# Chunked decay attention before a two-layer MLP and an expert layer: state, output and the next block's masked scores in one visit of TensorE

## The chip, the cores and the metric

One NeuronCore of a Trainium2 chip runs the whole program in one launch. The metric is the device time of that launch in microseconds (us). The engines are TensorE (PE; its weight loads are PEld), VectorE (DVE), ScalarE (ACT), GpSimd (POOL) and SyncE (SP, which here only issues loads).

## The reference

Three stages. The first is attention with a decay: for each head the sequence of 768 is cut into blocks, and a state of 64 x 64 per head runs through them.

```
intra = (q_b k_b^T * Dmask) v_b            # Dmask[i,j] = lam^(i-j) for i >= j
inter = (q_b * lam^(i+1)) kv_state
out_b = intra + inter
kv_state = lam^block * kv_state + (k_b * lam^(block-1-j))^T v_b
```

The second is an MLP over 1536 tokens, 512 to 2048 to 512, with the activation (h+1)^2/4 between -1 and 1, 0 below and h above. The third picks one of 8 experts for each token by the scaled dot product of the normalised token with the expert's embedding, applies a 512 to 1024 to 512 MLP with ReLU, and multiplies by the gate. The kernel uses blocks of 128, which gives the same function: 6 blocks for each of 2 sequences, 12 in all, m = 0 to 11. Blocks 0 and 6 start a sequence (cb = 0, no state comes in); blocks 5 and 11 end one (cb = 5, no state goes out).

## The kernel before, in words

**Order of work.** Layer 1 (the MLP) is a list of units (1, c, g): three chunks c of four blocks (512 tokens), eight groups g of 256 hidden columns. Units 0 to 7 are chunk 0, 8 to 15 chunk 1, 16 to 23 chunk 2; then come the expert tiles. In unit n TensorE does `m1_l1(n, 0)` and `m1_l1(n, 1)` (12 matmuls each, tile `l`), then the second layer of the unit before, `m1_l2(n - 1, j)` for j = 0 to 3 (6 matmuls each, tile `acc`). Every product is made of three matmuls, high and low halves of values and weights.

**Attention among the units.** Blocks 0 to 4 (`NSTART` = 5) run ahead of everything. Blocks 5 to 11 are needed by chunks 1 and 2 and are put between the matmuls of layer 1: `plan` holds functions by quarter steps, and `place(n, k)` runs them behind the first half (k = 0), the second half (1), the second layer's j = 1 (2) and j = 3 (3) of unit n. `attn_pieces` makes the pieces of a block: `prep` (GpSimd's kd and qd, and the loads of the next block on SyncE, L273 to L296), `masked` (score matmuls L308 in tile `sc`, mask multiplication L311 on VectorE to `am`), `outv` and `outs` (output matmuls L335 and L348 in tile `ao`, their eviction L354 on ScalarE and L355 on VectorE), `st` (state matmuls L377 in tile `as`, the new state L380 on ScalarE or four L383 on VectorE). `scores` is `prep` and `masked`. Blocks 5 to 7 are spread over steps 0.5 to 7.75, blocks 8 to 11 over 8.5 to 15.75, each as [scores, st, output, nothing].

**Who decides the order.** TensorE's order is the order in which the program issues it (`manual_schedule`). VectorE, ScalarE, GpSimd and SyncE get a fixed order when the program is compiled: a planner goes through a simulated time and takes for each engine the instruction earliest in the program whose inputs it thinks ready. On the chip each engine runs its list in order and waits where an input is late.

**Banks.** Accumulators `acc0` to `acc3` take four banks, `ps_l1` two (tag `l1`, the two halves of a layer-1 unit), `ps_at` two (tag `at`, all attention tiles and small ones). A layer-1 bank is free again when ScalarE has read it (L719, then L720 squares in place) and VectorE has made `g_t` from both (L722); `gh` (L726) and `gl` (L727) follow. `kd` and `qd` have two buffers each, `am` three; attention inputs have two buffers (`big_a`, `big_b`).

**Weights.** In chunk 0 the raw 8-byte weights are converted by ScalarE and VectorE (`convert`, L223 to L239; cu, cz, cw) and stored for the later chunks; `hilo` (L212, L213) splits them. For unit n this is issued ahead of the unit's matmuls. Chunk 0's tokens are scored against the experts during units 9 to 12 (L449 on VectorE, eight for each block, tile `jk` with the tag `kd`).

Of the kernel before, what the change touches and what calls it, by code (L numbers as in the profile page):

```python
# [8 lines left out]
F32 = mybir.dt.float32  # L9
# [8 lines left out]
P = 128  # L18
NTOK = 1536
DM = 512  # L20
NBLK = 12
NE = 8
TMAX = 13
CHUNKS = [4, 4, 4]
# [7 lines left out]

X2STEP = (1.0, 0.75)
ROUTE = (6.5, 4.5)
SPREAD = (0.5, 7.75)

WARM = 11
NSTART = 5
WARM_LAM = 6

SWAP = 7
# [6 lines left out]
def kernel(  # L48
# [15 lines left out]
    V, A, G, PE, SP = nc.vector, nc.scalar, nc.gpsimd, nc.tensor, nc.sync  # L64
# [8 lines left out]
    ps_l1 = ctx.enter_context(tc.tile_pool(name="ps_l1", bufs=2, space=bass.MemoryType.PSUM))  # L73
# [179 lines left out]
    first_blk = []  # L253
# [4 lines left out]
    ast = {}  # L258
    pieces = {}
# [3 lines left out]
    def at_tile(shape, name):  # L263
        if at_tags:
            pool, tag = at_tags.popleft()
            return pool.tile(shape, F32, name=name, tag=tag)
        return ps_at.tile(shape, F32, name=name, tag="at")

    def attn_pieces(m):
        c, j = blk_chunk[m]  # L270
        cb = m % 6

        def prep():  # L273
            if m >= NSTART - 1 and m + 1 < NBLK:
                load_attn(m + 1)
            qkt, kvt = attn_in[m]
            def keys():
                kd = sb.tile([P, NE, 64], F32, name="kd", tag="kd")
                G.tensor_tensor(kd, kvt[:, 0], rev.to_broadcast([P, NE, 64]), op=ALU.mult)
                ast[m, "kd"] = kd  # L280


            if cb < 5 and m >= NSTART:
                keys()
            if cb > 0:
                qd = sb.tile([P, 4, P], F32, name="qd", tag="qd")
                if m < SWAP:
                    G.tensor_tensor(qd, qkt[:, 0], wq, op=ALU.mult)
                else:
                    G.tensor_tensor(qd[:, 0::2, :], qkt[:, 0, 0::2, :], wq[:, 0::2, :], op=ALU.mult)  # L290
                    for h2 in range(2):
                        r, o = slice(64 * h2, 64 * h2 + 64), slice(64 - 64 * h2, 128 - 64 * h2)
                        G.tensor_tensor(qd[o, 1::2, :], qkt[r, 0, 1::2, :], wq[r, 1::2, :], op=ALU.mult)
                ast[m, "qd"] = qd
            if cb < 5 and m < NSTART:
                keys()  # L296

        def scores():
            prep()
            masked()  # L300

        def masked():
            qkt, kvt = attn_in[m]
            pts = [at_tile([P, 4, P], "sc") for _ in range(2)]
            for pr in range(4):
                for h2 in range(2):
                    r = slice(64 * h2, 64 * h2 + 64)
                    PE.matmul(pts[h2][:, pr, :], lhsT=qkt[r, 1, pr, :], rhs=qkt[r, 0, pr, :], start=True, stop=True)  # L308
            for h2 in range(2):
                am = sb3.tile([P, 4, P], F32, name="am", tag="am")  # L310
                ast[m, "am"] = V.tensor_tensor(am, pts[h2], dmask.rearrange("p (r o) i -> p r o i", o=2)[:, :, h2, :], op=ALU.mult)  # L311
                ast[m, "A", h2] = am

        def outv():
            kvt = attn_in[m][1]
            if j == 0:
                n = CHUNKS[c]
                xh[c] = sb.tile([P, 4, n * P], F32R, name="xh", tag="xh")
                xl[c] = sb.tile([P, 4, n * P], F32R, name="xl", tag="xl")
            am = [ast.pop((m, "A", i)) for i in range(2)]  # L320


            if m < SWAP:
                pt = at_tile([P, 4, P], "ao")
                pts, first, last = [pt[:, pr, :] for pr in range(4)], (0,), (3,)
                ast[m, "o"] = pts, [(pt, slice(0, 4))]
            else:
                two = [at_tile([P, 2, P], "ao") for _ in range(2)]
                pts, first, last = [two[pr % 2][:, pr // 2, :] for pr in range(4)], (0, 1), (2, 3)
                ast[m, "o"] = pts, [(two[i], slice(i, 4, 2)) for i in range(2)]  # L330
            ast[m, "last"] = last
            for pr in range(4):
                for h2 in range(2):
                    r = slice(64 * h2, 64 * h2 + 64)
                    PE.matmul(  # L335
                        pts[pr][r], lhsT=kvt[:, 1, 2 * pr + h2, :], rhs=am[h2][:, pr, :],
                        start=(pr in first), stop=(cb == 0 and pr in last), skip_group_check=True,
                    )

        def outs():  # L340
            pts, banks = ast.pop((m, "o"))
            last = ast.pop((m, "last"))
            if cb > 0:
                for pr in range(4):
                    for h2 in range(2):
                        r = slice(64 * h2, 64 * h2 + 64)
                        w = r if m < SWAP or pr % 2 == 0 else slice(64 - 64 * h2, 128 - 64 * h2)
                        PE.matmul(  # L348
                            pts[pr][r], lhsT=state[m - 1][w, pr, :], rhs=ast[m, "qd"][w, pr, :],
                            start=False, stop=(pr in last), skip_group_check=True,  # L350
                        )
            sl = slice(j * P, (j + 1) * P)
            for pt, prs in banks:
                ast[m, "xh"] = A.activation(xh[c][:, prs, sl], pt, AF.Copy)  # L354
                ast[m, "xl"] = V.tensor_tensor(xl[c][:, prs, sl], pt, xh[c].bitcast(F32)[:, prs, sl], op=ALU.subtract)  # L355

        def outp():
            outv()
            outs()

        def st():
            if m == NSTART:
                with tc.issue_after(ast[m, "am"].ins):
                    V.tensor_copy(lamx[:, 0::2], lamc[:, 0::2])
                    V.tensor_copy(lamx[64:128, 1::2], lamc[0:64, 1::2])
                    V.tensor_copy(lamx[0:64, 1::2], lamc[64:128, 1::2])
            if cb == 5:
                return
            qkt, kvt = attn_in[m]
            kd = ast.pop((m, "kd"))  # L370
            pt = at_tile([P, 4, 64], "as")
            for pr in range(4):
                for h2 in range(2):
                    h = 2 * pr + h2
                    at_ = 64 * h2 if m < SWAP - 1 or pr % 2 == 0 else 64 - 64 * h2
                    r = slice(at_, at_ + 64)
                    PE.matmul(pt[r, pr, :], lhsT=kd[:, h, :], rhs=kvt[:, 1, h, :], start=True, stop=True)  # L377
            sn = sb.tile([P, 4, 64], F32, name="s_new", tag="state")
            if cb == 0:
                A.activation(sn, pt, AF.Copy)  # L380
            else:
                for pr in range(4):
                    V.scalar_tensor_tensor(  # L383
                        sn[:, pr, :], state[m - 1][:, pr, :], (lamc if m < SWAP else lamx)[:, pr, :], pt[:, pr, :], op0=ALU.mult, op1=ALU.add,
                    )
            state[m] = sn

        pieces[m] = (prep, masked, outv, outs)
        return [scores, st, outp, None] if m >= NSTART else [scores, None, outp, st]


    def inv_norm(s, n, nm, over_=None):
# [440 lines left out]
    pcs = [attn_pieces(m) for m in range(NBLK)]  # L833
# [8 lines left out]
    for h2 in range(2):  # L842
        PE.matmul(
            lps[64 * h2:64 * h2 + 64, NE:NE + 4], lhsT=ident[:, P - 1:P].to_broadcast([P, 64]),
            rhs=rev.rearrange("p (r h) o -> p r (h o)", h=2)[:, :, h2], start=True, stop=True,
# [4 lines left out]
    for h2 in range(2):  # L850
        PE.matmul(
            wqp[64 * h2:64 * h2 + 64], lhsT=ident[:, P - 1:P].to_broadcast([P, 64]),
            rhs=dmask.rearrange("p (r o) i -> p r o i", o=2)[:, :, h2, :], start=True, stop=True,
# [25 lines left out]
    def at(step, *fs):  # L879

        s0 = round(4 * step)
        for i, f in enumerate(fs):
            if f:
                plan.setdefault(s0 + i, []).append(f)

    def spread(fs, s0, s1):
        for i, f in enumerate(fs):
            at(s0 + (s1 - s0) * i / len(fs), f)

    def place(n, k):  # L890
        now[0] = n + k / 4.0
        for f in plan.pop(4 * n + k, ()):
            f()
# [62 lines left out]
    for n in range(NU):  # L956
        lay, c, g = units[n]
        if lay == 1 and g == 0:
            if c + 1 < len(CHUNKS):
                m0 = first_blk[c + 1]  # L960
                fs = [f for m in range(max(m0, NSTART), m0 + CHUNKS[c + 1]) for f in pcs[m]]
                spread(fs, n + SPREAD[0], n + SPREAD[1])
            if c == 1:
                setup_routing()
        load_w(1, n + 2)
# [90 lines left out]
    with tc.If(lo_n < hi_n):  # L1056
        with tc.For_i(lo_n, hi_n) as i:
            e = SP.value_load(eti[0:1, bass.ds(i, 1)], min_val=0, max_val=NE - 1)
            dyn = []
            for nm, src in (("ixd", idx), ("rowd", row), ("gxd", gx)):  # L1060
                d = sb.tile([P, 2], I32, name=nm, tag=nm)
# [74 lines left out]
```

## Time and profile before

| | |
|---|---|
| Median of 3 runs | 476.63 us (474.26 to 476.95) |
| The profiled execution | 474.53 us, span of the instructions 472.7 us |
| TensorE | 463.7 us busy (98%), 2713 matmuls |
| VectorE | 326.7 us (69%) |
| ScalarE | 266.6 us (56%) |
| GpSimd | 82.4 us (17%) |
| Mean granted TensorE clock | 0.996 |

Rows of a timeline are: start, duration, engine, line, operation, output <- inputs, shape, count, and in brackets idle time before it with what ended it. Matmuls are pipelined: a row's duration is longer than its distance to the next, and distances are what counts. A 4-byte matmul of attention shows as two records, so eight matmuls are x16. A row of waits is: who <- whom, us in total, times, longest.

### The profile page before, as it was taken

The numbers are of one execution on the slowest core, as the hardware profiler recorded it, in microseconds if no ns is written. First come the engines' busy times: TensorE is split into PE (matmuls) and PEld (weight loads), VectorE is DVE, ScalarE is ACT, GpSimd is POOL, SyncE is SP. The second block draws the span as 40 slices with busy tenths as digits, with TensorE's granted clock in tenths as the row PEclk, the third lists the DMA queues.
The fourth block names the chain that finished last, engine by engine and source line by source line (L and its number), as shares of the span: only waits on it lengthen the run. The fifth ranks groups of instructions, "written<-read, shape, count | busy, mean of one in ns | idle before, by whom it ended". The sixth has DMA issues, their size and how long they took to land.

```text
span 472.7 us, 7356 instructions
## 1 busy us (share of the span) xinstructions
PE 463.7 (98%) x2713; PEld 377.7 (80%) x2713; DVE 326.7 (69%) x725; ACT 266.6 (56%) x403; POOL 82.4 (17%) x83
## 2 busy tenths in 40 slices
PE   8999999999999999999999999999999999999994
PEld 5875878878878787878888888887778889899882
DVE  6889889879399997474799875575794445435430
ACT  2388879868874454454665655556433534533521
POOL 4612420002003030000000005200055600500202
PEclk9999999999999999999999999999999999999998
DMA  8999987868563333122423325240275633543401
GB/s 327 420 411 367 392 305 287 298 231 251 230 220 137 97 128 116 63 90 90 178 67 125 122 90 179 90 155 23 88 250 178 201 136 109 179 155 98 146 1 50
DMA packets 22651, 83.65 MB, mean 177 GB/s; under 512 B 3595, under 2 KB 3595, under 8 KB 20564
## 3 DMA queue, kind: packets, MB, share of 16 engines
q1 hardware_dynamic: 15842, 65.04, 38.9%
q10 hardware_dynamic: 4322, 11.55, 6.2%
q0 software_dynamic: 2448, 6.56, 4.0%
q8 instruction: 22, 0.36, 0.3%
q14 instruction: 17, 0.14, 0.1%
HBM read 68.44 MB, written 14.73 MB: 176 GB/s over the span
## 4 chain that ended last, share of the span: by engine, by line
PE 68%; issue 20%; POOL 6%; DVE 3%; ACT 1%; POOLq 0%; another core or an unknown queue 0%; ACTq 0%
PE l L700 10%; PE acc L743 9%; PE l L702 9%; PE acc L744 9%; PE l L703 9%; PE acc L745 9%; POOL out_dram L823 2%; PE ao L335 2%; PE sc L308 2%; POOL xg L763 2%; POOL gate L771 2%; PE acc L738 1%; PE ao L348 1%; PE as L377 1%; PE m L794 1%
## 5 line engine op out<-in xcount | busy, mean ns | idle before, releaser
L213 DVE TENSOR_TENSOR w2l<-rw,w2h 128x1024 fp32r<-128x1024 f32 x32 | 39.1, 1223 | 55.1 <-ACT w2h L212 47.5
L700 PE MATMUL l<-xh,w1h 128*128 128x512 f32 x192 | 75.2, 397 | 0.7 <-ACT w1h L212 0.6
L743 PE MATMUL acc<-w2h,gh 128*128 128x512 f32 x184 | 72.8, 396 | 0.0
L703 PE MATMUL l<-xh,w1l 128*128 128x512 f32 x184 | 71.7, 390 | 0.0
L745 PE MATMUL acc<-w2h,gl 128*128 128x512 f32 x184 | 71.7, 390 | 0.0
L702 PE MATMUL l<-xl,w1h 128*128 128x512 f32 x184 | 71.7, 390 | 0.0
L744 PE MATMUL acc<-w2l,gh 128*128 128x512 f32 x184 | 71.7, 389 | 0.0
L212 ACT ACTIVATE w2h<-rw 128x1024 fp32r<-128x1024 f32 x32 | 33.9, 1059 | 57.0 <-PE m2a L819 30.0
L449 DVE CUSTOM_DVE_ANT_0 jk<-x2s,enb 128x512 f32<-128x512 f32 x72 | 48.1, 700 | 0.8 <-ACT x2s L434 0.6
L213 DVE TENSOR_TENSOR w1l<-rw,w1h 128x1024 fp32r<-128x1024 f32 x32 | 39.7, 1241 | 11.1 <-ACT w1h L212 10.2
L726 ACT ACTIVATE gh<-g_t 128x512 fp32r<-128x512 f32 x46 | 29.0, 630 | 32.1 <-DVE g_t L722 32.1
L719 ACT ACTIVATE r_t<-l,half 128x512 f32<-128x512 f32 x48 | 32.4, 679 | 25.6 <-PE l L703 25.1
L794 PE MATMUL m<-x2h,w1h 128*128 128x384 f32 (+2 forms) x128 | 43.9, 343 | 0.0
L700 PEld LDWEIGHTS l<-xh,w1h 128*128 128x128 f32 x192 | 35.9, 188 | 9.5 <-ACT w1h L212 1.2
L796 PE MATMUL m<-x2h,w1l 128*128 128x384 f32 (+2 forms) x128 | 43.3, 338 | 0.0
L795 PE MATMUL m<-x2l,w1h 128*128 128x384 f32 (+2 forms) x128 | 43.1, 337 | 0.0
L722 DVE SCALAR_TENSOR_TENSOR g_t<-r_t,l 128x512 f32<-128x512 f32 x46 | 31.4, 683 | 16.1 <-ACT r_t L720 16.0
L817 PE MATMUL m2a<-w2h,mh 128*128 128x512 f32 (+1 forms) x104 | 41.5, 399 | 0.0
L819 PE MATMUL m2a<-w2h,ml 128*128 128x512 f32 (+1 forms) x104 | 40.8, 392 | 0.0
L743 PEld LDWEIGHTS acc<-w2h,gh 128*128 128x128 f32 x184 | 34.5, 188 | 7.8 <-issue 0.5
L818 PE MATMUL m2a<-w2l,mh 128*128 128x512 f32 (+1 forms) x104 | 40.7, 391 | 0.0
L745 PEld LDWEIGHTS acc<-w2h,gl 128*128 128x128 f32 x184 | 34.5, 188 | 7.3
(250 smaller groups left out, 844.1 us busy)
## 6 DMA issues: line engine op xcount, KB each, us to landing
rw<-wsc SPq DMA_DIRECT2D x32, 512.0 KB, 3.1
rw<-in_w_dram SPq DMA_DIRECT2D x32, 512.0 KB, 3.2
rw<-in_w_in_dram SPq DMA_DIRECT2D x8, 1024.0 KB, 9.2
rw<-in_w_out_dram SPq DMA_DIRECT2D x8, 1024.0 KB, 9.6
wsc<-cw ACTq DMA_DIRECT2D x15, 512.0 KB, 6.7
qk_t<-in_qk_dram SPq DMA_DIRECT2D x12, 512.0 KB, 3.7
kv_t<-in_kv_dram SPq DMA_DIRECT2D x12, 512.0 KB, 6.7
x2d<-x2s ACTq DMA_DIRECT2D x12, 256.0 KB, 2.2
```

Of the source, the lines that this page charges most:

```text
L213: wlo[key] = eng.tensor_tensor(lo, r, hi.bitcast(F32), op=ALU.subtract)
L449: V.tensor_tensor_reduce(out=jk, in0=x2s, in1=enb[e // 2][:, e % 2, :], scale=1.0, scalar=0.0, op0=ALU.mult, op1=ALU.add, accum_out=lr[:, ...
L700: PE.matmul(pt, lhsT=hi[:, f, k, :], rhs=xh[c][:, k, :], start=(k == 0), stop=False)
L702: PE.matmul(pt, lhsT=hi[:, f, k, :], rhs=xl[c][:, k, :], start=False, stop=False)
L703: PE.matmul(pt, lhsT=lo[:, f, k, :], rhs=xh[c][:, k, :], start=False, stop=(k == 3))
L743: PE.matmul(a, lhsT=gh[:, f, sl], rhs=hi[:, f, :], start=(g == 0 and f == 0), stop=False)
L744: PE.matmul(a, lhsT=gh[:, f, sl], rhs=lo[:, f, :], start=False, stop=False)
L745: PE.matmul(a, lhsT=gl[:, f, sl], rhs=hi[:, f, :], start=False, stop=(g == 7 and f == 1))
L794: PE.matmul(pt, lhsT=hi[:, f, k, :], rhs=self.xh[:, k, :], start=(k == 0), stop=False)
L795: PE.matmul(pt, lhsT=hi[:, f, k, :], rhs=self.xl[:, k, :], start=False, stop=False)
L796: PE.matmul(pt, lhsT=lo[:, f, k, :], rhs=self.xh[:, k, :], start=False, stop=(k == 3))
L817: PE.matmul(a, lhsT=gh[:, f, sl], rhs=hi[:, f, :], start=(g == 0 and f == 0), stop=False)
```

## The change

The list [scores, st, output, nothing] spread over steps is gone. At step 0.5 the scores of block 5 are made as before. At steps 2.5, 4.5, 6.5, 8.5, 10.5, 12.5 and 14.5 (k = 2: between the second layer's j = 1 and j = 2) stands one `visit` of blocks 5 to 11: state matmuls, output matmuls with their eviction, the scores and masks of the next block, the new state, and the next block's `prep`. In a visit the scores take two tiles of `ps_l1` with the tag `l1`. From block 7 on (`SWAP`) the two output tiles are whole banks, and the state matmuls write the second half of one of them. The parts of a block are otherwise the same instructions.

```diff
-SPREAD = (0.5, 7.75)
+FIRST_SCORES = 0.5
+VISIT = {5: 2, 6: 4, 7: 6, 8: 8, 9: 10, 10: 12, 11: 14}
...
-        def masked():
+        def masked(behind_=False):
             qkt, kvt = attn_in[m]
-            pts = [at_tile([P, 4, P], "sc") for _ in range(2)]
+            if behind_:
+                pts = [ps_l1.tile([P, 4, P], F32, name="sc", tag="l1") for _ in range(2)]
+            else:
+                pts = [at_tile([P, 4, P], "sc") for _ in range(2)]
...
-                two = [at_tile([P, 2, P], "ao") for _ in range(2)]
+                two = ast.pop((m, "two"), None) or [at_tile([P, 4, P], "ao") for _ in range(2)]
                 pts, first, last = [two[pr % 2][:, pr // 2, :] for pr in range(4)], (0, 1), (2, 3)
-                ast[m, "o"] = pts, [(two[i], slice(i, 4, 2)) for i in range(2)]
+                ast[m, "o"] = pts, [(two[i][:, 0:2, :], slice(i, 4, 2)) for i in range(2)]
...
-        def outp():
-            outv()
-            outs()
-
         def st():
+            stp()
+            ste()
+
+        def stp():
...
-            pt = at_tile([P, 4, 64], "as")
+            if m < SWAP:
+                pt = at_tile([P, 4, 64], "as")
+            else:
+                two = ast[m, "two"] = [at_tile([P, 4, P], "ao") for _ in range(2)]
+                pt = two[1][:, 2:4, :].rearrange("p a (b d) -> p (a b) d", d=64)
+            ast[m, "st"] = pt
...
+
+        def ste():
+            if cb == 5:
+                return
+            pt = ast.pop((m, "st"))
             sn = sb.tile([P, 4, 64], F32, name="s_new", tag="state")
...
-        pieces[m] = (prep, masked, outv, outs)
-        return [scores, st, outp, None] if m >= NSTART else [scores, None, outp, st]
+        def visit():
+            stp()
+            outv()
+            outs()
+            if m + 1 < NBLK:
+                pieces[m + 1][1](True)
+            ste()
+            if m + 1 < NBLK:
+                pieces[m + 1][0]()
+
+        pieces[m] = (prep, masked, outv, outs, visit)
+        return [scores, None, None, st]
...
-            if c + 1 < len(CHUNKS):
-                m0 = first_blk[c + 1]
-                fs = [f for m in range(max(m0, NSTART), m0 + CHUNKS[c + 1]) for f in pcs[m]]
-                spread(fs, n + SPREAD[0], n + SPREAD[1])
+            if c == 0:
+                at(FIRST_SCORES, pcs[NSTART][0])
+                for m, u in VISIT.items():
+                    at(u + 0.5, pieces[m][4])
```

## Rows read from the trace of the kernel before

**Rows 1.** Stretches: us, busy us (count) by engine, PEclk, DMA share, GB/s

```profile
core 0: us, PE busy (x) PEld busy (x) DVE busy (x) ACT busy (x) POOL busy (x), PEclk, DMA share, GB/s
...
47.30:58.30 11.00, 11.00 (x50) 9.11 (x49) 8.73 (x10) 8.77 (x12) 5.65 (x6) 1.00 0.99 389
58.30:109.25 50.95, 50.95 (x305) 40.73 (x304) 44.39 (x53) 41.48 (x54) 6.68 (x6) 1.00 0.79 287
130.00:183.00 53.00, 53.00 (x340) 42.13 (x340) 52.42 (x130) 29.66 (x51) 9.34 (x8) 1.00 0.41 140
```

**Rows 2.** Waits of TensorE's matmuls from 25.2 to 217 us, all of them

```profile
PE l L700 <- ACT w1h L212: 0.6, 1, 0.6
```

**Rows 3.** Timeline of TensorE around the scores of block 6

```profile
60.13 0.39 PE L703 MATMUL l<-xh,w1l 128*128 128x512 f32 x1
...
60.81 0.39 PE L703 MATMUL l<-xh,w1l 128*128 128x512 f32 x1
61.13 1.16 PE L308 MATMUL sc<-qk_t 64*128 64x128 f32 x16
62.22 0.50 PE L700 MATMUL l<-xh,w1h 128*128 128x512 f32 x1
62.56 0.39 PE L702 MATMUL l<-xl,w1h 128*128 128x512 f32 x1
```

**Rows 4.** Timeline of TensorE: the state of block 6, the output of block 7

```profile
67.89 0.69 PE L377 MATMUL as<-kv_t,kd 128*64 128x64 f32 x16
68.50 0.50 PE L743 MATMUL acc<-w2h,gh 128*128 128x512 f32 x1
...
104.78 1.09 PE L335 MATMUL ao<-am,kv_t 128*64 128x128 f32 x16
105.80 0.67 PE L348 MATMUL ao<-qd,s_new 64*64 64x128 f32 x16
106.40 0.50 PE L743 MATMUL acc<-w2h,gh 128*128 128x512 f32 x1
```

**Rows 5.** Timeline of TensorE at the start: attention matmuls one behind the other

```profile
13.92 0.69 PE L377 MATMUL as<-kv_t,kd 128*64 128x64 f32 x16
14.44 1.04 PE L335 MATMUL ao<-am,kv_t 128*64 128x128 f32 x16
15.41 1.40 PE L308 MATMUL sc<-qk_t 64*128 64x128 f32 x16
```

**Rows 6.** Timeline, unit 2: its last first-layer matmul, and VectorE behind it

```profile
52.65 0.39 PE L703 MATMUL l<-xh,w1l 128*128 128x512 f32 x1
...
55.30 1.22 DVE L232 SCALAR_TENSOR_TENSOR cw<-cz,cu 128x1024 int32<-128x1024 int32 x1 [0.34 <-DMA wsc<-cw]
...
59.40 0.68 DVE L722 SCALAR_TENSOR_TENSOR g_t<-r_t,l 128x512 f32<-128x512 f32 x1
```

**Rows 7.** Timeline, units 6 and 10: last first-layer matmul, g_t of that half

```profile
101.74 0.39 PE L703 MATMUL l<-xh,w1l 128*128 128x512 f32 x1
...
108.65 0.68 DVE L722 SCALAR_TENSOR_TENSOR g_t<-r_t,l 128x512 f32<-128x512 f32 x1
...
151.11 0.39 PE L703 MATMUL l<-xh,w1l 128*128 128x512 f32 x1
...
156.92 0.68 DVE L722 SCALAR_TENSOR_TENSOR g_t<-r_t,l 128x512 f32<-128x512 f32 x1
```

**Rows 8.** Waits of VectorE from 58.3 to 109.25 us, the one for state matmuls

```profile
DVE s_new L383 <- PE as L377: 2.5, 1, 2.5
```

**Rows 9.** Timeline, block 9: the matmul after its scores, and its first mask

```profile
152.52 0.50 PE L743 MATMUL acc<-w2h,gh 128*128 128x512 f32 x1
...
156.31 0.69 DVE L311 TENSOR_TENSOR am<-sc,dmask 128x512 f32<-128x512 f32 x1
```

**Rows 10.** Waits of SyncE's load queue for attention's buffers, whole span

```profile
SPq L102 <- PE sc L308: 22.0, 5, 7.7
SPq L105 <- PE ao L335: 16.7, 5, 9.4
```

**Rows 11.** Stretch after the last matmul, columns as in rows 1

```profile
466.40:472.60 6.20, 0.00 (x0) 0.00 (x0) 0.00 (x0) 0.68 (x1) 0.87 (x1) 0.70 0.09 31
```

## Prediction before the run

> [...]
>
> **What is saved: entries and exits.** Layer-1 matmuls start every (60.81 - 60.13) / 3 = 0.227 us. A score stay takes 62.56 - 60.81 = 1.75 us from the last layer-1 matmul before it to the second one after it; two spacings of that are 0.45, so it costs 1.30, of which its own matmuls are 62.22 - 61.13 = 1.09. The remaining 0.21 is the price of one entry and exit [rows 3]. Before there are 19 stays of blocks 5 to 11: seven of scores, five of state, seven of output, by the code. After there are eight: the scores of block 5 and seven visits. 11 x 0.21 = 2.3 us. A state alone takes 68.50 - 67.89 = 0.61 [rows 4], but 14.44 - 13.92 = 0.52 when output matmuls follow at once [rows 5]: 5 x 0.09 = 0.45. Together 2.8 us. Against it stands one row of the start, where scores straight behind attention matmuls take 1.40 instead of 1.16 [rows 3, 5]; if that were the price of the seam, six visits would lose 6 x 0.24 = 1.4 and 1.3 would be left. I take 2.8, since I read the 0.24 as a wait for a bank, and banks come next. No matmul is added or removed.
>
> **What is added: two waits on layer-1 banks.** There are only two such banks. At a visit they hold the two halves of the unit just computed, and the scores can start only when VectorE has made g_t (L722) from both. Between the unit's last layer-1 matmul and the scores TensorE has 12 second-layer matmuls (2.72), the entry (0.09), state 0.52, and output 1.02 + 0.60 [rows 4]: 4.95 us.
>
> Visit 5, in unit 2: the unit's last layer-1 matmul starts at 52.65 and is through at 52.88; g_t ends at 59.40 + 0.68 = 60.08, because VectorE first converts weights and waits for a store of converted weights to leave their buffer [rows 6]. That is 7.2 us. Block 5 has no state, so cover is 2.72 + 0.09 + 1.62 = 4.4 and the wait at least 2.8. The upper end comes from TensorE's place in the work: scores of block 6 end at 62.22 today [rows 3], with 24 layer-1 and second-layer matmuls (5.44) done that the change puts behind them. Unhindered it would be there at 62.22 - 5.44 - 0.21 = 56.57; released at 60.08 it is there at 60.08 + 1.09 = 61.17, 4.6 late. (The output of block 5 moves from step 1.75 to this visit, so TensorE comes earlier, but VectorE, paced by the DMA engines, does not.) I take 4.0, near the upper end for that reason. Queued behind the waiting scores are the other 12 second-layer matmuls and all of the next unit.
>
> Visits 6 and 7: in unit 6 the last layer-1 matmul is through at 101.97 and g_t at 109.33, 7.36 us later [rows 7], 2.4 over the cover. But VectorE itself lost 2.5 us of that stretch waiting for the state matmuls of block 7 [rows 8], which now come before the scores, and it has 4.0 us in hand once TensorE has waited at visit 5. I take 0; the bounds are 0 and 2.4 each.
>
> Visits 8 to 10, while VectorE is full: in unit 10 the bank is free at 156.92 + 0.68 = 157.60, 6.26 us after 151.34 [rows 7]; 6.26 - 4.95 = 1.3. A full VectorE does not catch up by being left alone, but a wait once paid is paid. I take 1.3 in all, between 0 and 3 x 1.3 = 3.9.
>
> The other wait is at the far end: the next unit's first half needs the bank back from the mask multiplication (L311). Behind a visit lie 12 matmuls and the exit, 2.83 us. The masks of block 9 show the danger: the first ends at 156.31 + 0.69 = 157.00, 4.48 us after its scores were done at 152.52 [rows 9]; 1.65 over. In the unit of the first wait VectorE is only 79% to 87% busy [rows 1], and the multiplication follows at once. I take 1.0 for the full stretch, between 0 and 3 x 1.65 = 5.0.
>
> **What moves and costs nothing.** SyncE's loads of block m+2 have waited 22.0 us in all for score matmuls and 16.7 us for output matmuls to free their buffers, with weight loads queued behind [rows 10], and yet TensorE waited 0.6 us for a weight [rows 2]. Now both loads stand behind a visit that has just freed both buffers, and their block is used two units later: 0, between -0.6 and the 9.4 us that one such wait has lasted, spread over weights that are fetched two units ahead. GpSimd's kd and qd are made a visit ahead and have two units of cover. kd now holds one of two buffers for two units while VectorE's score junk (jk, L449) uses that tag; nothing reads the junk, so one buffer will do. The state additions (L383) come after the masks and are needed a visit later.
>
> **Sum.** -2.8 + 4.0 + 1.3 + 1.0 = +3.5 us. The profiled execution took 474.53 us, 472.7 of it span; the 1.8 outside it is untouched: 478.0. The median shown, 476.63, is 2.1 above that execution; on its footing the forecast is 480.1.
>
> **Rivals.**
> *The waits stay away.* The order of VectorE and ScalarE is planned anew around the changed TensorE order, and g_t may land earlier in it. For it: 6.6 us of VectorE's 50.95 us in units 3 to 6 are idle [rows 1]. Against it: weights come before g_t in the program, and in unit 2 the delay comes from the DMA engines. Then -2.8: 473.8 on the median's footing.
>
> *The lag returns at every visit.* If the 7 us are the order of the work and not a backlog, a pause of TensorE delays ScalarE and VectorE too, and each visit pays: 4.0, half of 2.4 at visit 6, 2.4 at visit 7, 3 x 1.3, and the 1.0: 12.5 - 2.8 = +9.7, 486.3. Visit 7 decides: were its scores to start 2 us after the output, this is it. For it: all three lags shown (units 2, 6 and 10) exceed 4.9 [rows 6, 7]. Against it: the 2.5 us of [rows 8].
>
> [...]
> [...]
>
> **How the numbers follow.** The forecast has 0.45, the waits that stay away 0.27, the lag at every visit 0.16, the clock 0.12. About 1%, 4.8 us, can be told from no change: below 471.9 or above 481.4. Faster needs the first rival and 2 us more: 0.05. Slower takes three tenths of the forecast (bounds of 1.3 and 1.0 above what I took), nearly all of the second rival and two thirds of the third: 0.36. The rest, 0.59, is the same. The range runs from 473.0, below the first rival, to 486.5; the forecast's own is 477 to 484.
>
> **What would show it.** The profile after has eight stays; state, output and scores follow each other within 0.2 us where no bank is waited for. In the table of waits TensorE's scores wait for VectorE's g_t, most of it at the first visit, 3 to 4 us, near 57 us of the span; there may be a second entry, layer-1 matmuls waiting for the masks. The clock stays 1.00. [...]

## The result, and the profile after

The changed kernel takes 482.48 us (median of 4 executions, 480.70 to 482.73), the kernel before 475.94 beside it (4 executions, 474.26 to 476.95). The ratio is 1.0146, with a 95% interval of 1.0122 to 1.0171: slower by 6.5 us. The profiled execution of after took 480.70 us, span 478.9: 6.2 more than the one that the prediction was worked out from (474.53).

Nearly all of it lies in layer 1. There the first layer-1 matmul starts at 24.95 us (before: 25.20) and the first one of unit 16 at 229.03 (before: 222.61): 204.1 us in place of 197.4, by the same 1142 matmul records. So 6.7 us come in between; 0.25 of earlier start comes off, and the way from unit 16 to the end is 0.2 shorter (249.9 us; before: 250.1).

First the waits of TensorE's matmuls from 25 to 218 us in after, all of them (who <- whom, us in total, times, longest); [rows 2] had one line here:

```profile
PE l L724 <- DVE am L315: 2.9, 2, 1.8
PE l L724 <- DVE g_t L746: 2.5, 1, 2.5
PE rkp L527 <- DVE xl L359: 0.9, 1, 0.9
PE sc L312 <- DVE g_t L746: 0.7, 1, 0.7
PE l L724 <- ACT w1h L213: 0.6, 1, 0.6
```

Four of the five are new, and only one is the wait that the prediction put first, that of the scores for g_t. Layer 1's own matmuls wait for both things that VectorE does to those banks: g_t before a visit and the masks (am) behind it. The stretches show where; they answer to [rows 1] and have its columns, the second and third a little longer at the end:

```profile
47.30:58.30 11.00, 8.50 (x61) 6.47 (x59) 10.46 (x11) 8.34 (x12) 1.44 (x2) 1.00 0.99 382
58.30:112.00 53.70, 52.88 (x325) 43.07 (x324) 45.85 (x53) 42.12 (x56) 7.92 (x6) 1.00 0.77 269
130.00:190.00 60.00, 57.12 (x391) 46.05 (x391) 54.61 (x133) 34.77 (x60) 7.06 (x7) 1.00 0.36 119
```

TensorE, which filled every one of these before, is idle for 2.50 us of the first, 0.82 of the second and 2.88 of the third. The granted clock is 1.00 in all three.

**A stay with no wait.** TensorE's timeline of after at the visit of block 7:

```profile
107.32 0.39 PE L769 MATMUL acc<-w2h,gl 128*128 128x512 f32 x1
107.64 0.69 PE L386 MATMUL ao<-kv_t,kd 128*64 128x64 f32 x16
108.16 1.05 PE L339 MATMUL ao<-am,kv_t 128*64 128x128 f32 x16
109.13 0.67 PE L352 MATMUL ao<-qd,s_new 64*64 64x128 f32 x16
109.73 1.19 PE L312 MATMUL sc<-qk_t 64*128 64x128 f32 x16
110.84 0.50 PE L767 MATMUL acc<-w2h,gh 128*128 128x512 f32 x1
111.18 0.40 PE L768 MATMUL acc<-w2l,gh 128*128 128x512 f32 x1
```

From start to start: state 0.52, output 0.97 and 0.60, scores 1.11, and 0.20 more than two spacings of 0.227 for entry and exit together. That is what the prediction read from [rows 3 to 5]. The scores behind an output take 1.11 here, so the 1.40 of the start is not the price of a seam; that it was a wait for a bank, as the prediction read it, is not shown.

**The first visit.** The same view at unit 2:

```profile
43.15 1.88 PE L762 MATMUL acc<-w2f,gh 128*128 128x512 f32 x4
44.46 0.79 PE L724 MATMUL l<-xh,w1h 128*128 128x512 f32 x1
45.09 0.39 PE L726 MATMUL l<-xl,w1h 128*128 128x512 f32 x1
...
47.38 0.39 PE L727 MATMUL l<-xh,w1l 128*128 128x512 f32 x1
50.27 0.50 PE L724 MATMUL l<-xh,w1h 128*128 128x512 f32 x1 [2.50 <-DVE g_t L746]
...
55.95 1.09 PE L339 MATMUL ao<-am,kv_t 128*64 128x128 f32 x16
...
57.99 0.48 PE L312 MATMUL sc<-qk_t 64*128 64x128 f32 x2
59.15 1.16 PE L312 MATMUL sc<-qk_t 64*128 64x128 f32 x14 [0.67 <-DVE g_t L746]
60.23 0.50 PE L767 MATMUL acc<-w2h,gh 128*128 128x512 f32 x1
```

and VectorE beside it:

```profile
47.87 1.74 DVE L214 TENSOR_TENSOR w2l<-cw,w2h 128x1024 fp32r<-128x1024 f32 x1
49.53 0.68 DVE L746 SCALAR_TENSOR_TENSOR g_t<-r_t,l 128x512 f32<-128x512 f32 x1
...
58.41 0.68 DVE L746 SCALAR_TENSOR_TENSOR g_t<-r_t,l 128x512 f32<-128x512 f32 x1
```

VectorE lags here much as the prediction read from [rows 6] (g_t ends 6.0 us behind the unit's last layer-1 matmul, 7.2 there), but TensorE meets the lag earlier. The second half of unit 2 needs a bank that g_t of unit 1 frees at 49.53 + 0.68 = 50.21, since VectorE prepares weights first: 50.27 - 47.38 - 0.23 = 2.66 late. Then the scores of block 6 wait for the last g_t of unit 2, 58.41 + 0.68 = 59.09: from 57.99 to 60.23 they take 2.24, 1.15 more than the 1.09 of [rows 3]. This place costs 3.8.

The expectations below count another 0.40 here, as a wait for a weight, because the first layer-1 matmul of unit 2 is listed at 44.46 and the next one at 45.09. The rows show no such wait: the four matmuls before, on the raw weights `w2f`, start 0.43 apart, so from 43.15 they take until 44.86, and 45.09 is one spacing of 0.227 later. The listed 44.46 lies within the last of the four.

**The masks.** TensorE and VectorE of after behind visit 8, where unit 9 begins:

```profile
136.12 0.50 PE L767 MATMUL acc<-w2h,gh 128*128 128x512 f32 x1
...
138.75 0.39 PE L769 MATMUL acc<-w2h,gl 128*128 128x512 f32 x1
140.95 0.50 PE L724 MATMUL l<-xh,w1h 128*128 128x512 f32 x1 [1.81 <-DVE am L315]
```

```profile
135.51 1.21 DVE L751 TENSOR_TENSOR gl<-g_t,gh 128x512 fp32r<-128x512 f32 x1
136.65 1.23 DVE L473 CUSTOM_DVE_ANT_0 jk<-x2s,enb 128x512 f32<-128x512 f32 x1
...
137.80 1.22 DVE L751 TENSOR_TENSOR gl<-g_t,gh 128x512 fp32r<-128x512 f32 x1
138.94 0.41 DVE L359 TENSOR_TENSOR xl<-ao,xh 128x256 fp32r<-128x256 f32 x1
139.28 0.68 DVE L473 CUSTOM_DVE_ANT_0 jk<-x2s,enb 128x512 f32<-128x512 f32 x1
...
140.22 1.27 DVE L315 TENSOR_TENSOR am<-sc,dmask 128x512 f32<-128x512 f32 x2
```

The scores are done at 136.12, but the masks start at 140.22, 4.1 us later. VectorE is never idle in between: it does two expert scores (jk) that nobody waits for yet, and three of its operations last 1.2 instead of 0.68 us, beside GpSimd's qd (135.18 to 138.46 us). Layer 1 starts at 140.95, 1.97 after its turn. The same happens at unit 11 with 1.22 (the masks start 3.3 us behind the scores there), so the masks cost 3.2.

**The rest.** The scores of blocks 7 to 11, in visits 6 to 10, take 0.62, 0.02, 0.12, 0.50 and 0.14 us longer than 1.09: 1.4. And at step 14.5 two things now stand at the same place, visit 11 and the routing of chunk 0 (`chunk_routed`), whose tile needs an attention bank that VectorE has to empty of block 11's output first (L359 in the list of waits, 0.9): 1.0. The sum of what is added is 3.8 + 3.2 + 1.4 + 1.0 = 9.4; 6.7 were lost, so 2.7 were saved. This last number is what is left over, not a measurement of its own.

### The profile page after: what moved, and what is told of

It is laid out like the page before. It is cut to its first block, busy times and chain, and to the rows that moved or that the text cites. A ratio compares the mean times of both kernels' runs of the same rounds, so it can differ in the third digit from the quotient of the medians.

```text
span 478.9 us, 7361 instructions
## 1 busy us (share of the span) xinstructions
PE 463.0 (97%) x2713; PEld 379.1 (79%) x2713; DVE 332.5 (69%) x725; ACT 266.4 (56%) x403; POOL 82.3 (17%) x83
## 4 chain that ended last, share of the span: by engine, by line
PE 40%; issue 19%; DVE 8%; POOL 5%; ACT 3%; POOLq 0%; another core or an unknown queue 0%
PE acc L767 5%; PE acc L768 5%; PE acc L769 5%; PE l L724 5%; PE l L726 5%; PE l L727 5%; DVE jk L473 3%; POOL out_dram L847 2%; PE m L818 1%; PE m L820 1%; PE m L819 1%; POOL gate L795 1%; POOL xg L787 1%; DVE w1l L214 1%; ACT sqs L452 1%
## 5 line engine op out<-in xcount | busy, mean ns | idle before, releaser
L751 DVE TENSOR_TENSOR gl<-g_t,gh 128x512 fp32r<-128x512 f32 x46 | 33.7, 733 | 11.4 <-ACT gh L750 11.2
```

## The experiments

The theory after this reading: the change gains what the prediction says, and loses it because layer-1 banks serve two users, with VectorE between them on both sides. The rivals: the lost time comes from GpSimd's work beside VectorE, which stands at the visit too, or from the fall of block 5's output out of step 1.75, or from TensorE's clock. Changes are shown against after.

**1. `scores_apart`: state and output in one stay, scores by themselves in attention's banks.**

```diff
-            if m + 1 < NBLK:
-                pieces[m + 1][1](True)
...
                     at(u + 0.5, pieces[m][4])
+                    if m + 1 < NBLK:
+                        at(u + 1.5, pieces[m + 1][1])
```

> State and output of a block stay together at step u + 0.5; the scores of the next block go back to attention's own two banks, in a stay of their own one unit later. Theory (the loss is the two waits on layer 1's banks): the waits for g_t at the scores and for the masks at layer 1 are gone, 8.8 us of the changed kernel's 9.8 us of added waits; the 1.0 us of the routing matmuls behind block 11's output stays, since that visit is unchanged. 14 stays instead of 19 save 5 x 0.21 + 5 x 0.09 = 1.5 us, so with the 1.0 the time is within 1 us of the kernel before: ratio 0.997 to 1.001. Rival (the loss comes from where the blocks and their loads now stand among the units, and from VectorE's order): the loss mostly stays, ratio 1.008 or more.

476.16 us, ratio to before 1.0021 (1.0004 to 1.0037): a little above the 0.997 to 1.001 of the theory, far from the rival's 1.008. All waits for masks and of the scores are gone; beside the 0.6 of [rows 2] these of TensorE are left:

```profile
PE l L722 <- DVE g_t L744: 2.0, 1, 2.0
PE rkp L525 <- DVE xl L359: 0.9, 1, 0.9
```

So the scores in layer 1's banks are what most of the loss hangs on, but not all: unit 2's second half still waits 2.0 for g_t, which the theory had not foreseen, and the routing 0.9. These two belong to the other parts of the change. From the first layer-1 matmul to unit 16 this version takes 200.2 us, 2.8 more than before: 1.5 saved by 14 stays in place of 19 at the prediction's prices (5 x 0.21 + 0.45), and 2.0, 0.9 and the 1.7 that follow added make 3.1. And something new appears, in the stretches around that wait of 2.0 us:

```profile
44.00:49.60 5.60, 3.67 (x15) 2.37 (x13) 5.60 (x6) 3.87 (x5) 4.18 (x3) 1.00 0.98 367
49.95:53.30 3.35, 3.35 (x9) 2.67 (x8) 3.25 (x4) 3.35 (x5) 0.75 (x1) 0.50 1.01 422
53.40:60.00 6.60, 6.60 (x53) 5.22 (x52) 5.03 (x7) 4.73 (x8) 0.00 (x0) 1.00 1.01 411
```

Behind the wait the granted clock is 0.50 for 3.35 us, with nine matmul records in them; by an estimate from 0.50 and 3.35 us (half of the time) the fall costs 1.7 us. So the clock, to which the prediction gives a chance of 0.12, does fall inside the work here, behind a wait of layer 1 for g_t.

**2. `pool_later`: the loads stay in the visit, GpSimd's part of `prep` goes to step u + 1.5.**

```diff
-                pieces[m + 1][0]()
+                pieces[m + 1][5]()
...
+                        at(u + 1.5, pieces[m + 1][6])
...
```

> The changed kernel with one part moved: GpSimd's kd and qd of the next block are issued one unit after the visit instead of at its end; the loads stay. Theory A (the masks are late because GpSimd's work of 3 us falls on VectorE's queue just ahead of them: its instructions there last 1.1 to 1.2 us instead of 0.68): the two waits of layer 1 for the masks, 1.96 and 1.22 us, shrink to under 1 us together, ratio to the kernel before 1.008 to 1.010. Theory B (the masks are late because the expert scores and evictions stand ahead of them in VectorE's order): these waits stay at 2.5 us or more, ratio 1.013 to 1.016.

480.49 us, 1.0103 (1.0071 to 1.0136). In the profile the waits for masks are 2.0 us in three places instead of 2.9 in two, between what the two theories had. It doesn't decide: only kd moved. GpSimd's qd, the longer part, still ran ahead of the masks (from 135.55 and 162.16 us), where the order planned for GpSimd put it.

**3. `out5_apart`: block 5's output back at step 1.75.**

```diff
-            outv()
-            outs()
+            if m > NSTART:
+                outv()
+                outs()
...
+                at(1.75, lambda: [pieces[NSTART][i]() for i in (2, 3)])
```

> The changed kernel with block 5's output back at step 1.75, a stay of its own; step 2.5 holds only the scores of block 6. Theory (what ends the first wait is VectorE's g_t of unit 2, at about 59 us, whatever TensorE does before): the wait of unit 2's second half for g_t, 2.65 us, shrinks by about 2 us and the wait at the scores of block 6, 1.15 us, grows by about as much; both with the weight wait together stay at 3.5 to 4.5 us and the time is that of the changed kernel, ratio 1.013 to 1.018. Rival (the wait is new because block 5's output was moved, so that TensorE came too early): together under 2 us, ratio 1.011 or less.

484.93 us, 1.0191 (1.0158 to 1.0225): above the 1.013 to 1.018 of the theory, and slower than after. The wait moved as the theory has it: unit 2's second half no longer waits, the scores of block 6 do, 3.9 us in two (TensorE's waits):

```profile
PE sc L312 <- DVE g_t L747: 3.9, 2, 2.5
```

The 2.0 us of block 5's output at step 1.75 were cover for g_t; without them the same debt to VectorE is paid a half unit earlier, with them at the scores. Most of the extra time (208.4 us from the first layer-1 matmul to unit 16, after 204.1) is the clock, which falls during the second of the two waits:

```profile
53.00:59.60 6.60, 3.91 (x18) 2.79 (x16) 6.08 (x6) 5.50 (x9) 1.31 (x1) 1.00 1.02 423
59.60:66.30 6.70, 5.47 (x22) 4.57 (x23) 6.68 (x9) 5.00 (x6) 0.00 (x0) 0.50 0.55 215
```

That is twice as long at 0.50 as in the first experiment, some 2.7 us by an estimate (half of the 5.47 us in which TensorE was busy there). All four executions have a mean clock of 0.986 to 0.989 over the span, the first four of after 0.992 to 0.996 and the five of `after_again` 0.990 to 0.994, so this is the kernel and not one execution.

**4. `visit_later`: each visit a quarter step later, behind all of the unit's second-layer matmuls.**

```diff
-                    at(u + 0.5, pieces[m][4])
+                    at(u + 0.75, pieces[m][4])
```

> The changed kernel with all visits one quarter later, behind the second layer's j = 3. Theory (two banks squeezed from both sides): the scores have 2.7 us more cover and never wait for g_t, but between them and the next unit's first half nothing is left, so that layer 1 waits for the masks at each of six visits, 1 us where VectorE is idle and 3 to 5 us where it is full: 12 to 20 us in place of the 7 of this kind of the changed kernel; ratio 1.025 to 1.045. Rival (only the g_t side matters, since the masks are short): ratio 1.000 to 1.010.

490.48 us, 1.0310 (1.0276 to 1.0345). TensorE's waits:

```profile
PE l L724 <- DVE am L315: 10.9, 6, 2.5
PE l L724 <- DVE g_t L746: 1.5, 1, 1.5
```

The ratio lies in the theory's range. The scores never wait for g_t now, and layer 1 waits for masks behind all six visits that make scores. This is the squeeze from two sides: twelve matmuls more ahead of the scores are twelve fewer behind the masks, and neither of the two places tried has room for both. The profiled execution was the fastest (486.68 us, mean clock 0.994); the other four took 489.46 to 490.85 at 0.985 to 0.988. It too has a stretch at 0.50, behind the mask wait of unit 9 (144.2 to 147.5 us).

**5. `out_merged`: the first experiment, block 5's output at step 1.75 as in the third, and the routing a quarter step later.**

```diff
-ROUTE = (6.5, 4.5)
+ROUTE = (6.75, 4.5)
```

> State and output of blocks 6 to 10 in one stay, their scores apart in attention's own banks, block 5's output back at step 1.75, the routing matmuls one quarter later (6.75), all else as in the changed kernel. Theory (all that the change lost were bank waits and what they did to the clock): no wait of TensorE over 0.5 us between 35 and 220 us but the one for a weight that the kernel before has too, the clock stays 1.00, and five entries fewer than before save 1.5 to 2.5 us: ratio 0.994 to 0.998. Rival (merging saves nothing that can be measured, since the seams inside a stay cost what the entries did): ratio 0.999 to 1.003.

473.09 us, 0.9958 (0.9940 to 0.9976): faster than both kernels, by 0.4% against the one before, as the theory has it. Beside the 0.6 of [rows 2] TensorE has one wait from 25 to 218 us:

```profile
PE acc L761 <- DVE w2f L233: 0.5, 1, 0.5
```

It is a wait of unit 0's second layer for its raw weights; of the changed kernel's two profiles one has it too (`after_again`, 0.4), the other not. The routing's wait is gone with the quarter step. The rest is the merging alone: 14 stays in place of 19, by the prediction's prices 1.5 us; measured 1.8 in the medians (474.84 beside it), and 1.1 in the profiles from the first layer-1 matmul to unit 16 (196.3 against 197.4), which with the 0.5 is 1.6.

**6. `filled`: after, and ten matmuls of 512 columns ahead of unit 2's second half, into a tile that nobody reads, in the time in which TensorE waits there.**

```diff
+        if n == 2 and f == 1:
+            fill = at_tile([P, nt], "fill")
+            for k in range(10):
+                PE.matmul(fill, lhsT=hi[:, 0, 0, :], rhs=xh[c][:, 0, :], start=True, stop=True)
```

> The changed kernel with ten matmuls of 512 columns, whose result nobody reads, in the place where unit 2's second half waits 2.65 us for its bank (block 5's output no longer stands before it). Theory (in most executions the granted clock falls to 0.5 for 3.4 us behind that wait, which costs 1.7 us on top of it; the one that was profiled was spared): TensorE works through the wait, the end of unit 2 stays where VectorE lets it, the clock never falls there, and the median is 1 to 2 us below that of the changed kernel run beside it. Rival (the clock has no part in the changed kernel's time; its executions differ by something else): the same median within 0.5 us, or later by up to 0.5.

481.37 us, 1.0139 (1.0111 to 1.0168). The wait of 2.5 us is no longer among TensorE's waits, the clock is 1.00 from 30 to 220 us of the profile, and the median is that of after in the same comparison (481.33, experiment 8), as the rival has it. The five executions of either spread over 1.9 to 2.6 us, so this rests on the medians; they show no sign that a fall of the clock behind that one wait is what makes after slow.

**7. `masks_first`: the expert scores of chunk 0 (jk) three quarters of a step later, and issued behind a block's masks.**

```diff
-                        at(n + 1 + X2STEP[c1] * j, lambda p_=p_: [f() for f in p_])
+                        if c1 == 0:
+                            def late(p_=p_, b={0: 9, 1: 10, 2: 10, 3: 11}[j]):
+                                with tc.issue_after(ast[b, "am"].ins):
+                                    for f in p_:
+                                        f()
+                            at(n + 1.75 + X2STEP[c1] * j, late)
...
```

> The changed kernel with the expert scores of chunk 0 (L473, eight on VectorE for each block) 0.75 step later and queued behind the masks of the visit before them. Theory B (masks come late since other work of VectorE stands ahead of them): the two waits of layer 1 for masks, 1.96 and 1.22 us, shrink to under 1.0 us together, 1.015 of the changed kernel becomes 1.008 to 1.011. Theory A (GpSimd slows VectorE there): they stay above 2 us.

477.74 us, 1.0063 (1.0043 to 1.0084): 3.6 below after in the same comparison, where the masks had cost 3.2, and better than the 1.008 to 1.011 of theory B. No layer-1 matmul waits for masks any more. VectorE's order changed elsewhere too: at unit 2 layer 1 waits 0.9 and the scores 2.0 for g_t, in place of 2.5 and 0.7. GpSimd's qd ran beside VectorE here too (136.54 to 139.74 us). VectorE:

```profile
136.53 1.83 DVE L751 TENSOR_TENSOR gl<-g_t,gh 128x512 fp32r<-128x512 f32 x2
138.27 0.74 DVE L359 TENSOR_TENSOR xl<-ao,xh 128x256 fp32r<-128x256 f32 x2
138.94 1.27 DVE L315 TENSOR_TENSOR am<-sc,dmask 128x512 f32<-128x512 f32 x2
```

So the masks were late because of their place on VectorE's list, behind work for which nobody waits. Beside GpSimd's qd the two gl took 1.83 us here, 0.92 each, where one took 0.68 without it (57.81 us in after), and yet layer 1 did not wait. How much of the wait would go if GpSimd's work alone were moved is not shown: at unit 9 of after three operations took 0.54 us longer each beside it, 1.6 in all, and the wait was 1.97.

**8. `after_again`: the changed kernel once more.**

> The changed kernel once more, beside the others. Theory: median 1.2% to 1.7% above the kernel before; the profiled execution either shows the clock at 1.00 and lies 1.5 to 2 us under the median, or shows a fall to 0.5 behind a wait and lies at the median. Rival: it lies at the median with the clock at 1.00.

481.33 us (480.94 to 482.81), 1.0134 (1.0106 to 1.0161). Its profiled execution is the slowest, 482.81, where the theory had one with a fall of the clock at the median. It came to layer 1 2.1 us later than the first one (27.03 against 24.95). A stretch of the start shows where, first in the profile of after, then here:

```profile
4.60:10.50 5.90, 5.73 (x87) 4.07 (x87) 4.96 (x14) 2.47 (x4) 2.73 (x3) 1.00 1.01 399
```

```profile
4.60:10.50 5.90, 5.90 (x41) 4.11 (x39) 4.06 (x13) 1.28 (x1) 2.08 (x2) 1.00 0.98 383
```

TensorE is busy throughout, but gets through 41 matmul records in place of 87. The clock column reads 1.00 here in both profiles; what set the slower pace is not shown.

The profile also shows a clock fall, behind the wait for masks of unit 9:

```profile
143.70:147.00 3.30, 3.30 (x9) 2.60 (x8) 3.27 (x9) 0.00 (x0) 0.00 (x0) 0.50 0.32 88
```

while in the first execution the same wait, as long (1.8), left the clock at 1.00 (130 to 190 us of after). The mean clock here is 0.994, as in `scores_apart` with its one stretch at 0.50, so by an estimate from the means the wait of 2.0 at unit 2 had no fall behind it. From the first layer-1 matmul to unit 16 both take the same, 204.0 and 204.1: this one had one mask wait fewer and a shorter wait at unit 2.

**9 and 10. `stay_freed` and `out_merged_2`.** The first keeps the change's idea where it can have room: one stay for blocks 6 to 11 with the scores in layer 1's banks, `masks_first`, block 5's output at 1.75, block 6's scores in attention's banks, and the routing of the fifth experiment. The second is the fifth once more, beside it. Of the first one's edit this is the line that the others don't have:

```diff
-                pieces[m + 1][1](True)
+                pieces[m + 1][1](m > NSTART)
```

> One stay for each of blocks 6 to 11 as in the changed kernel, scores in layer 1's banks, with each wait taken away: block 5's output back at step 1.75 and the scores of block 6 in attention's own banks at step 2.5, expert scores of chunk 0 later and behind the masks, the routing matmuls one quarter later. Theory (the one stay is worth its entries, and the waits are all that it cost): waits of TensorE on layer 1's banks under 1 us together, clock at 1.00 from 6 us to the last matmul, nine stays in place of the 14 of the kernel with only state and output merged: 1 us less than that kernel, ratio to the kernel before 0.992 to 0.996. Rival (the scores in layer 1's banks cannot be had for nothing: once one wait is gone, VectorE is late at another): waits of 2 us or more in all, ratio 0.998 or more.

> The kernel with only state and output merged, again beside the one before it: ratio 0.994 to 0.998, no wait on layer 1's banks. If the single stay with its waits taken away is worth its entries, this one is 0.5 to 1.5 us above it; if not, it is equal or below.

474.00 us, 0.9973 (0.9952 to 0.9994), and 473.38 us, 0.9973 (0.9955 to 0.9992). Neither is faster than the other by more than the intervals, where 0.5 to 1.5 us in favour of `stay_freed` had been expected; its ratio lies between the theory's 0.992 to 0.996 and the rival's 0.998. With nine stays it should save (14 - 9) x 0.21 = 1.05 on `out_merged`. Its timeline of TensorE at the visit of block 6 shows where that went:

```profile
81.05 0.48 PE L312 MATMUL sc<-qk_t 64*128 64x128 f32 x2
82.78 1.16 PE L312 MATMUL sc<-qk_t 64*128 64x128 f32 x14 [1.25 <-DVE g_t L747]
83.87 0.50 PE L768 MATMUL acc<-w2h,gh 128*128 128x512 f32 x1
```

From 81.05 to 83.87 these scores take 1.73 us more than 1.09. One wait for g_t costs more than five stays are worth: from the first layer-1 matmul to unit 16 `stay_freed` takes 197.4 us, as the kernel before, and `out_merged` 196.3 in both of its profiles.

## Why the prediction was right or wrong

The sign, the mechanism and the range held (480.1 in 473.0 to 486.5; measured 482.48), but the size was short: +3.5 forecast on the profiled execution, +6.2 measured, which carries the result from "within 1%", the likeliest outcome at 0.59, over to slower by over 1%, which had 0.36. The medians flatter it a little: 480.1 is 2.4 short of 482.48, but the kernel before was at 475.94 in the comparison and not at 476.63, so that 3.0 of its 6.5 us are missing. The sum puts TensorE's pauses in layer 1 into the end time one for one; 6.7 us more there and 6.2 at the end, with the 0.25 and 0.2 us before and behind it, bear that out.

**Saved, -2.8.** Held: 2.7 is what is left when the added waits are taken off, and `out_merged` gained 1.5 to 1.8 where the same prices give 1.5. Dismissing the 0.24 of the seam was right (1.11 at visit 7).

**Visit 5, +4.0.** The size held (3.8), the place only in part. The step that failed is the one on block 5's output: it moves, so TensorE comes earlier, but VectorE does not. That is right, and was not followed to the first matmul that meets it. That is the second half of unit 2, which waited 2.7, and only 1.15 was left for the scores. `out5_apart` shows it from the other side. One number in the working was off as well: the cover of 4.4 takes block 5's output at the 1.62 of block 7, but it takes 2.04 (55.95 to 57.99), which would have lowered "at least 2.8" to 2.35.

**Visits 6 and 7, 0, and 8 to 10, +1.3.** Measured 0.6, and 0.8. Visit 7, from which the second rival was to be decided, shows 0.02: the lag doesn't return at every visit. The prediction's reason, that VectorE's wait for state matmuls [rows 8] lengthened the lag of unit 6, fits the shorter lag there (4.9 us after, 7.36 before), but was not tried by itself.

**Masks, +1.0.** This is the term that was mis-sized: 3.2, inside its bounds of 0 to 5.0. The prediction saw the danger in [rows 9] (1.65 at one visit), then took a fifth of the upper bound, without asking what else VectorE's list would hold between scores and masks. Its own [rows 1] said that VectorE is busy 52.42 of 53.00 us there; work that nobody waits for is in that number, and `masks_first` shows that its place in the list, with the same amount of work, is what made layer 1 wait; GpSimd's share in it is not separated.

**What costs nothing.** SyncE waits 6.6 us for scores and 21.8 for outputs to free attention's buffers, where [rows 10] has 22.0 and 16.7, and the one listed wait of TensorE for a weight stayed 0.6 (the second execution adds 0.4): held. But the list of moved things lacked one that had stayed put: the routing at step 14.5, next to which visit 11 now stands. Its 1.0 us for an attention bank was in no bound; it is visible in the code alone, and `out_merged` removes it by a quarter step.

With 3.2 and 1.0 in place of 1.0 and 0 the prediction's sum is -2.8 + 4.0 + 1.3 + 3.2 + 1.0 = +6.7, the 6.7 us measured from the first layer-1 matmul to unit 16. That it meets to the tenth is luck: the other three terms, -2.7 + 3.8 + 1.4 by measurement, are each off a little and cancel, and the 2.7 is itself what the sum leaves over.

**The clock, 0.12.** The chances count a fall of the clock as the third rival, with two thirds of its 0.12 in the 0.36 for slower. No run had shown a fall inside the work then, nor what one costs; the runs since show falls to 0.50, of 1.7 and some 2.7 us by estimate. "The clock stays 1.00" held in the profiled execution of after (1.00 from 25 to 230 us), and not as a rule. Of the eight profiles whose longest wait is 1.8 to 2.5 us five show one stretch at 0.50 (`scores_apart`, `out5_apart`, `visit_later`, `masks_first`, `after_again`), two none (after, `filled`); of `pool_later` only the mean is known, 0.994, as in `scores_apart`, `visit_later` and `after_again`. Before, `out_merged` and `stay_freed`, where the longest wait is 1.2, show none; the mean of `out_merged_2` is 0.998, that of `out_merged`. The 1.7 us are those of `scores_apart`; the stretch of `out5_apart`, twice as long, costs the 2.7. In `masks_first` the four executions with a mean clock of 0.994 and above took 477.1 to 477.4 us, the four below 478.1 to 479.4. For after itself no share of the median is shown: `filled` gains nothing, and the nine executions of after don't order by their mean clocks.

**What stays open.** Behind which waits the clock falls; why TensorE got through 41 matmul records in place of 87 from 4.6 to 10.5 us of one execution; how much of the mask waits is GpSimd's; and whether a version with nine stays and no wait at all would beat `out_merged`, since none was tried.

## What to carry to other kernels

A bank that is lent to a second user needs room on two sides: its first user's last reader must be done before the loan, and the second's before the return. Add both lags (here 5 to 7 us for g_t, and 3.3 and 4.1 for the masks) and compare the sum with all the work that lies around the loan (here 4.95 and 2.83); if it doesn't fit, shifting the visit moves the wait from one side to the other (`visit_later` lost by it), and an order in which the readers come first gains (`masks_first`). Then ask of each item that a fully busy engine does in that gap whether anybody waits for it, and of each place to which work is moved what stands there already.

## What the runs showed of the hardware

While GpSimd's multiplications of qd ran (135.18 to 138.46 us in after), three operations of VectorE on 128 x 512 elements (gl, jk, gl, from 135.51 us on) took 1.21, 1.23 and 1.22 us, where an expert score (jk) took 0.68 just behind (139.28). In that stretch it is three times 0.54 us, a little more than the 1.4 that two expert scores took alone.

The granted clock was 0.50 for 3.3 to 3.4 us inside the work in four profiles (`scores_apart` 49.95 to 53.3 us, `masks_first` 59.2 to 62.6, `after_again` 143.7 to 147.0, `visit_later` 144.2 to 147.5) and for 6.7 us in a fifth (`out5_apart`, 59.6 to 66.3); in the stretch behind each it was 0.99 or 1.00. Before each fall TensorE had one of its longest waits in layer 1 (1.8 to 2.5 us); in `out5_apart` it was still in it. The wait for the masks of unit 9, 1.8 us in both executions of the changed kernel, had a fall behind it in `after_again` and none in after.
